# Value means from GpSimd's sums, two casts moved to VectorE, one block of the first x on ScalarE, and one hash a slot earlier, in a fused hash attention and SwiGLU kernel

## The chip, the cores and the metric

The kernel runs on one core of a Trainium2 chip. Such a core has five engines that work side by side, each with an instruction stream of its own in program order: TensorE (PE in the profile; its weight loads are listed as PEld), VectorE (DVE), ScalarE (ACT), GpSimd (POOL) and SyncE (SP), which here only issues DMAs. The engines wait for each other by semaphores. The metric is the device time of one execution, in microseconds. "The median" is that of three runs; the profile is one more execution.

## The reference

```
q, k, v: (4, 8, 768, 64)     batch, heads, sequence, head size; fp32
proj: (64, 6)                w_gate, w_val: (512, 1536)   w_out: (1536, 512)   rms_g: (512,)

bits(t)  = (t @ proj > 0)                        # six bits of each query and key
bucket   = sum(bits * 2**arange(6))
mask     = q_bucket[:, None] == k_bucket[None, :]
scores   = where(mask, q @ k.T / 8, -1e9)
p        = exp(scores - max);   attn = p / (sum(p) + 1e-9)
x        = (attn @ v), the 8 heads side by side          # (3072, 512)
xn       = x / sqrt(mean(x*x) + 1e-6) * rms_g
out      = (silu(xn @ w_gate) * (xn @ w_val)) @ w_out    # (3072, 512)
```

## The kernel before

**Mask.** Nothing is masked by comparison. Each query and key of a head gets six (or twelve) more rows beside its 64 numbers, plus or minus a constant for each hash bit. The product of these rows is largest where all bits agree, so one matmul gives scores in which every other bucket lies far down and vanishes in the exponential. A tile `QK` holds a pair of heads: rows 0 to 63 are the numbers in fp16 (written by casts), the rows from 64 on the hash rows; columns 0 to 767 are queries, the rest keys.

**Means.** A query whose bucket is empty must get the mean of the values, which the small constant `C0` brings in: `v_mean` multiplies the values by a matrix of ones, which sums over the 128 partitions and (with six matmuls into one PSUM bank) over the six blocks of keys, and DVE writes the result, scaled, into `cvb`. Where GpSimd has already added up the six blocks (`v_sum`, into `vsum`), one matmul does. `attn_out` adds `cvb` to the weighted sums before it divides. Before the change batches 0 and 1 use six matmuls for each pair of heads, and batches 2 and 3 use one on GpSimd's sums.

**Units and slots.** A unit `u` is half the queries (384) of a batch; there are eight. A slot is a third of a head: two scores matmuls (L321), one exponential on ACT (`probs`, L333). A unit has 24 slots. The whole program is one list of slots, written out by hand: `at(w, s, f, ...)` appends a step to slot 24*w + s. In slot t the loop emits `scores` of slot t+1, `probs` of slot t, and then the steps of the list in the order in which they were appended. A scores tile has two buffers. The weighted sums (`av`, L346, 18 matmuls a head in two parts) come some slots after their head, into the only bank of their kind; `attn_out` (DVE, then GpSimd) takes them out.

**Filling.** While unit u's attention runs, PE also does unit u-1's gate and value products (`gate`, `value`, L425) and unit u-2's output product (`project`, L454). `spread` lays these pieces over the slots by rough costs (SCORES, AV, PROJ and so on), and puts in the hash of a pair (`hash_one`) at its slot, at the next start of a whole piece. All these matmuls, the hashes (`d_ps`), the transposes of x (`x_ps`) and the means (`m_ps`) share three PSUM banks (`gps`), in rotation. A gate's bank comes free when DVE's first product has read it (L442, `a`), a value's when the second has (L443, `ht`).

**Heads.** Up to pair (1, 1) (batch 1, heads 2 and 3) queries and keys are loaded in rows, turned on PE (`turn_pe`), copied out by DVE or ACT (L152), cast to `QK` on GpSimd (L166), hashed by `hash_direct`, and their hash rows are moved into place by DVE (L251) or sent by DMAs on SP (`send_pair`: L258, then L261). The later pairs are loaded in blocks (`load_blocks`, eight DMAs, and `load_v`, one; all on SP), turned on DVE (`turn_dve`, L176 and L183), cast on GpSimd (L196) and hashed by `hash_one`: eight matmuls (L204), the signs (L212), two selects (L219) and four DMAs on SP (L280). The table `spots` gives for each of these pairs the slot of its load, of its key turns, its query turns and its hash. The casts follow one slot after the turns, and the values' cast and sums (`v_prep`, L289; `v_sum`, L295 to L297) two slots after the last turn; steps that would fall into slots 2 to 6 of a unit move to slot 7. Loaded tiles share eight buffers in rotation, so a load waits until the tile eight before it has been read for the last time. SP works through its DMAs in program order.

**The start.** Pair 0 of batch 0 is set up ahead of the slots: its first head is hashed, and `second_head` (slot 0) does the signs and moves of the second. In slot 1 follow the cast of its values and that of the second half of its queries, both on GpSimd. Units 0 and 1 take turns here: heads 0 and 1 of both come first (`order`).

**The first x.** After the last head of unit 0 a chain runs with nothing beside it that PE could do: the sums are taken out on DVE, squared and reduced (L360 to L388), GpSimd takes the power (L392), DVE scales x (`norm`, L401), PE turns its three blocks (`turn_x`, L408) in slot TX = 37, DVE multiplies them by the weights of the norm (L414), and only then does the first gate matmul start. `turn_x` can also do the multiplication as four on ACT (L412), as it does for one block of the last unit.

Of the kernel before, what the change touches and what calls it, by code (L numbers as in the profile page):

```python
# [31 lines left out]
def kernel(  # L32
# [12 lines left out]
    nc = tc.nc  # L45
# [31 lines left out]
    vls = [const.tile([128, H, 6, 66], FP16, name=f"vl{i}") for i in range(2)]  # L77
# [82 lines left out]
    def turned(b, hp, which):  # L160
        return (qT if which == "q" else kT)[b, hp].rearrange("p (h c) -> p h c", h=2)

    def cast_part(b, hp, which, e, h0=0, n=2):

        o = (0 if which == "q" else S) + e * HALF
        nc.gpsimd.tensor_copy(  # L166
            QK[b, hp][0:64, h0 : h0 + n, o : o + HALF],
            turned(b, hp, which)[64 * e : 64 * e + 64, h0 : h0 + n, :],
        )
# [113 lines left out]
            )  # L283


    def v_prep(b, hp):
        vn = raw[b, hp][2]
        hs = slice(2 * hp, 2 * hp + 2)
        nc.gpsimd.tensor_copy(vls[b % 2][:, hs, :, 0:64], vn)  # L289

    def v_sum(b, hp):
        vn = raw[b, hp][2]
# [244 lines left out]
    NS = 24  # L537
# [5 lines left out]
    def at(w, s, f, *a):  # L543
        plan[NS * w + s].append(lambda: f(*a))
# [7 lines left out]
    sign, move, _ = hash_direct(0, 0, (0,))  # L552
# [9 lines left out]
    sign1, move1, _ = hash_direct(0, 0, (1,))  # L562
# [29 lines left out]
        moves[b, hp][1]()  # L592

    at(0, 0, second_head)
    at(0, 1, v_prep, 0, 0)
    at(0, 1, cast_part, 0, 0, "q", 1)
    for hp, s0 in ((1, 2), (2, 7), (3, 13)):
        at(0, s0, new_pair, 0, hp)
        at(0, s0, turn_pe, 0, hp, 0, "k")
        at(0, s0 + 1, turn_pe, 0, hp, 1, "k")  # L600
        at(0, s0 + 1, cast_pool, 0, hp, "k")
        at(0, s0 + 2, turn_pe, 0, hp, 0, "q", nc.scalar.copy)
        at(0, s0 + 3, turn_pe, 0, hp, 1, "q", nc.scalar.copy)
        at(0, s0 + 3, cast_pool, 0, hp, "q")
        at(0, s0 + 4, hash_pair, 0, hp)
        at(0, s0 + 6, move_pair, 0, hp, 0)
        at(0, s0 + 8, move_pair, 0, hp, 1)
    at(0, 1, load_natural, nc.sync, 0, 3, "k")
    at(0, 1, load_natural, nc.sync, 0, 3, "q")
    at(0, 2, load_v, nc.sync, 0, 2)  # L610
# [12 lines left out]
    for hp, ts in ((0, (8, 22, 23, 24, 25, 24, 26, 26, 28, 42)), (1, (12, 27, 28, 29, 30, 29, 41, 32, 33, 43))):  # L623
        tl, ts = ts[0], ts[1:]
        for w in "kq":
            at(0, tl, load_natural, nc.sync, 1, hp, w)
        at(0, tl, load_v, nc.sync, 1, hp)
        at(0, ts[0], new_pair, 1, hp)
        for t, hh, w in zip(ts[0:4], (0, 1, 0, 1), "kkqq"):
            at(0, t, turn_pe, 1, hp, hh, w)  # L630
        at(0, ts[4], cast_pool, 1, hp, "k")
        at(0, ts[5], cast_pool, 1, hp, "q")
        if hp == 0:
            at(0, ts[6], hash_pair, 1, hp)
            at(0, ts[7], send_pair, 1, hp)
        at(0, ts[8], v_prep, 1, hp)
        at(2, 3 + 6 * hp, v_mean, 1, hp, 2, range(6))

    spots = {
# [11 lines left out]
    TX = 37  # L651
# [8 lines left out]
    at(0, 24, nc.gpsimd.tensor_scalar_mul, gcol, gcol, float(DMODEL) ** 0.5)  # L660
    for n, (u, h) in enumerate(order):
        for part in range(2):
            at(0, 3 * n + 4 + part, av, u, h, part)
        if h % 2:
            if (u, h) == (0, H - 1):

                at(0, 3 * n + 5, o_step, u, h // 2, nc.vector)
                at(0, 3 * n + 5, s_step, u, h // 2)
                at(0, 3 * n + 5, norm_scale, u)
                at(0, 3 * n + 6, hash_only, 1, 1)  # L670
                at(0, 3 * n + 6, hash_signs, 1, 1)
                at(0, 3 * n + 6, norm, u)
                at(0, 3 * n + 7, send_pair, 1, 1)
                at(0, TX - 1, idle, 2, bank)
                at(0, TX, idle, 1, bank)
                for c in range(3):
                    at(0, TX, turn_x, u, c)
                continue
            at(0, 3 * n + 5, o_step, u, h // 2)
            at(0, 3 * n + (10 if h < 7 else 7), s_step, u, h // 2)  # L680
# [1 line left out]

    SCORES, AV, PROJ, FEED, TURN, HASH = 330, 290, 216, 324, 220, 1000
    hashes = {spot[3]: (HASH, hash_one, *pair) for pair, spot in spots.items()}

    def spread(t0, n, pieces):
        fixed = [SCORES + (AV if (t - 1) % 3 < 2 else 0) for t in range(t0, t0 + n)]
        extra = [(t, *hashes.pop(t)) for t in range(t0, t0 + n) if t in hashes]  # L690
        total = sum(fixed) + sum(p[0] for p in pieces) + sum(e[1] for e in extra)
        i, done = 0, 0
        for s in range(n):
            done += fixed[s]
            while i < len(pieces):
                weight, whole, steps = pieces[i]
                if extra and whole and t0 + s >= extra[0][0]:
                    _, weight, *step = extra.pop(0)
                    at(0, t0 + s, *step)
                    done += weight  # L700
                    continue
                if done + weight // 2 > total * (s + 1) // n:
                    break
                done += weight
                for delay, *step in steps:
                    at(0, t0 + s + delay, *step)
                i += 1
        for _, _, *step in extra:
            at(0, t0 + n - 1, *step)
        assert i == len(pieces)  # L710

    for u in range(7):
# [4 lines left out]
        if u == 0:  # L717
            t0 = TX + 1
            spread(t0, 2 * NS - t0, gates)
            continue  # L720
        t0 = NS * (u + 1)
        at(0, t0 + 4, norm, u)
        pieces = []
        for i in range(9):
            c, n = divmod(i, 3)
# [6 lines left out]
                    (TURN, False, [(0, turn_x, u, c)]) for c in ((0,), (1, 2))[i - 6]  # L732
                ]
        spread(t0, NS, pieces + gates)
    for t, (_, *step) in hashes.items():
        at(0, t, *step)

    def behind_norm(t):
# [3 lines left out]
    for (b, hp), (load, kturns, qturns, _) in spots.items():  # L742
        at(0, load, load_blocks, nc.sync, b, hp)
        at(0, load, load_v, nc.sync, b, hp)
        at(0, kturns[0], new_pair, b, hp)
        for w, turns in (("k", kturns), ("q", qturns)):
            for i, t in enumerate(turns):
                at(0, t, turn_dve, b, hp, w, i, len(turns))
            at(0, behind_norm(turns[-1] + 1), cast_pool, b, hp, w)
        t = behind_norm(qturns[-1] + 2)  # L750
        at(0, t, v_prep, b, hp)
        if b > 1:
            at(0, t, v_sum, b, hp)
            at(2 * b, 3 + 6 * hp, v_mean, b, hp, 2)
        else:
            at(2 * b, 3 + 6 * hp, v_mean, b, hp, 2, range(6))


    def head_of(t):
# [61 lines left out]
```

## Time and profile before

| | us |
|---|---|
| median of three runs | 343.63 (342.87 to 345.09) |
| profiled execution | 344.45 |
| its span in the trace | 342.6 |
| PE busy | 329.6 |
| DVE busy | 249.2 |
| ACT busy | 225.6 |
| GpSimd busy | 146.3 |

| group | count | mean ns of one |
|---|---|---|
| scores matmul, 384 columns (L321) | 384 | 326 |
| mean matmul, 130 columns, from the values (L305) | 48 | 220 |
| mean matmul, 130 columns, from GpSimd's sums (L305) | 8 | 225 |
| cast of values on GpSimd (L289) | 16 | 846 |
| the three additions of GpSimd's sums (L295, L296, L297) | 8 each | 1002, 458, 457 |
| multiplication of a turned block of x on DVE (L414) | 23 | 686 |
| the same on ACT, a quarter of a block (L412) | 4 | 369 |

The span is the time from the first to the last instruction of the trace; the execution's own time also holds what lies around it. A matmul's listed time is its way through the pipe. Matmuls overlap, so what one costs PE is the distance from its start to that of the next one: four of 384 columns take 0.65 us, though each is listed with some 0.33. A line of the timeline gives the start, the time that a run of equal instructions takes, the engine, the line of the code and the shapes, how many they are, and in brackets how long the engine sat idle before and what ended that.

### The profile page before, as it was taken

What the parts mean: (1) busy time and instruction counts of PE and PEld (TensorE: products, weight loads), DVE (VectorE), ACT (ScalarE), POOL (GpSimd) and SP (SyncE); (2) the same over time, 40 slices, a digit from 0 to 9 for tenths busy, and PEclk for the clock granted to TensorE, in tenths of its full rate; (3) what the DMA queues carried; (4) which work ended last, traced back from release to release, by engine and by line L of the source; (5) the groups of instructions that cost most, each with busy time, mean ns of one, the idle gap of its engine ahead of it and who ended that gap; (6) DMA issues with size and microseconds to landing.
All of it is one profiled execution on the core that took longest, in us unless ns stands there. A gap on an engine that the chain in (4) does not pass through costs nothing.

```text
span 342.6 us, 7811 instructions
## 1 busy us (share of the span) xinstructions
PE 329.6 (96%) x3030; PEld 197.7 (58%) x3030; DVE 249.2 (73%) x523; ACT 225.6 (66%) x327; POOL 146.3 (43%) x208
## 2 busy tenths in 40 slices
PE   7798989999989999999999999999999999999996
PEld 3465746656656556654656556565556656664554
DVE  3689996778878758976799757986696546674870
ACT  3789866666747667767676667776667867753322
POOL 4589927125343532737362623637281121112000
PEclk9999999999999999999999999999999999999999
DMA  7999947912957017161727027100200010001002
GB/s 228 331 199 287 208 96 118 201 39 45 198 115 140 4 68 151 45 125 50 122 77 140 5 70 129 50 5 26 76 4 6 3 61 33 0 2 61 33 0 94
DMA packets 79029, 31.21 MB, mean 91 GB/s; under 512 B 64928, under 2 KB 75024, under 8 KB 78992
## 3 DMA queue, kind: packets, MB, share of 16 engines
q1 hardware_dynamic: 75888, 25.73, 31.3%
q0 software_dynamic: 2656, 4.72, 7.8%
q8 instruction: 24, 0.39, 0.5%
q10 hardware_dynamic: 448, 0.27, 0.3%
q14 instruction: 13, 0.11, 0.1%
HBM read 28.32 MB, written 6.29 MB: 101 GB/s over the span
## 4 chain that ended last, share of the span: by engine, by line
PE 84%; DVE 10%; ACT 2%; issue 2%; POOL 1%; DMA 1%; DVEq 0%; SPq 0%; POOLq 0%
PE v_ps L425 17%; PE g_ps L425 17%; PE s_ps L321 16%; PE y_ps L454 16%; PE o_ps L346 9%; PE d_ps L204 2%; PE t_ps L150 2%; PE d_ps L229 2%; PE x_ps L408 1%; ACT psb L333 1%; DVE xnT L414 1%; PE m_ps L305 1%; DVE a L442 1%; PE z_ps L525 1%; DVE QK L251 1%
## 5 line engine op out<-in xcount | busy, mean ns | idle before, releaser
L333 ACT ACTIVATE psb<-s_ps,ebias 128x768 f16<-128x768 f32 x192 | 168.1, 901 | 24.3 <-PE s_ps L321 23.5
L321 PE MATMUL s_ps<-QK 76*128 76x384 f16 (+1 forms) x384 | 93.8, 326 | 4.4 <-DVE QK L251 1.9
L433 ACT ACTIVATE t<-g_ps 128x384 f32<-128x384 f32 x96 | 47.2, 491 | 61.7 <-PE g_ps L425 60.9
L425 PE MATMUL g_ps<-xnT,wg 128*128 128x384 f16 x384 | 82.5, 325 | 1.0 <-DVE xnT L414 0.8
L425 PE MATMUL v_ps<-xnT,wv 128*128 128x384 f16 x384 | 81.6, 325 | 0.9 <-DVE a L442 0.8
L442 DVE SCALAR_TENSOR_TENSOR a<-t,g_ps 128x384 f32<-128x384 f32 x96 | 52.7, 548 | 26.9 <-ACT t L433 25.1
L454 PE MATMUL y_ps<-wo,ht 128*128 128x512 f16 x276 | 68.0, 378 | 0.0
L367 POOL TENSOR_TENSOR x<-otmp,rcp 128x384 f32<-128x384 f32 x31 | 25.7, 830 | 98.8 <-DVE rcp L365 98.3
L346 PEld LDWEIGHTS <-psb 128*128 128x128 f16 x1152 | 51.9, 97 | 18.3 <-issue 2.3
L443 DVE SCALAR_TENSOR_TENSOR ht<-a,v_ps 128x384 f16<-128x384 f32 x96 | 53.2, 554 | 11.5 <-PE v_ps L425 2.5
L346 PE MATMUL o_ps<-vl,psb 128*128 128x65 f16 x1152 | 56.3, 193 | 1.0 <-DVE otmp L360 0.9
L321 PEld LDWEIGHTS <-QK 76*128 76x128 f16 (+1 forms) x384 | 34.4, 98 | 37.2 <-issue 11.3
L425 PEld LDWEIGHTS <-wv 128*128 128x128 f16 x384 | 35.2, 97 | 23.3 <-issue 2.5
L425 PEld LDWEIGHTS <-wg 128*128 128x128 f16 x384 | 34.7, 97 | 21.9 <-issue 0.9
L454 PEld LDWEIGHTS <-ht 128*128 128x128 f16 x276 | 24.7, 97 | 22.5
L196 POOL CAST QK<-kT 64x768 f16<-64x768 f32 x20 | 16.4, 822 | 24.9 <-DVE kT L176 11.5
L372 POOL TENSOR_TENSOR sq<-x 128x384 f32<-128x384 f32 x31 | 25.7, 828 | 2.4
L466 ACT COPY ysb<-y_ps 128x512 f32<-128x512 f32 x23 | 13.5, 586 | 18.5 <-PE y_ps L454 18.4
L196 POOL CAST QK<-qT 64x768 f16<-64x768 f32 x20 | 16.6, 831 | 19.3 <-DVE qT L183 18.0
L376 DVE TENSOR_REDUCE ssp<-sq 128x3 f32<-128x384 f32 x32 | 16.9, 529 | 9.7 <-POOL sq L372 9.6
L360 DVE TENSOR_TENSOR otmp<-o_ps,cvb 128x390 f32<-128x390 f32 x32 | 17.9, 558 | 5.9 <-PE o_ps L346 5.6
L414 DVE TENSOR_TENSOR xnT<-x_ps,gcol 128x512 f16<-128x512 f16 x23 | 15.1, 686 | 5.9 <-PE x_ps L408 5.9
(76 smaller groups left out, 275.2 us busy)
## 6 DMA issues: line engine op xcount, KB each, us to landing
vn<-in_v_dram SPq DMA_DIRECT2D x16, 384.0 KB
out_dram<-ysb SPq DMA_DIRECT2D x23, 256.0 KB
qL<-in_q_dram SPq DMA_DIRECT2D x40, 96.0 KB
kL<-in_k_dram SPq DMA_DIRECT2D x40, 96.0 KB
kn<-in_k_dram SPq DMA_DIRECT2D x5, 384.0 KB
qn<-in_q_dram SPq DMA_DIRECT2D x5, 384.0 KB
wg<-in_moe_w_gate_dram POOLq DMA_DIRECT2D x2, 768.0 KB, 10.2
wv<-in_moe_w_val_dram POOLq DMA_DIRECT2D x2, 768.0 KB, 9.7
```

What stands on the lines that cost most here:

```text
L196: nc.gpsimd.tensor_copy(QK[b, 2 * hp + hh, "h"][0:64, o : o + S], src[64 * hh : 64 * hh + 64, :])
L321: nc.tensor.matmul(ps[:, j, 0:HALF], QK[b, h, "h"][0:rows, S + jt * 128 : S + (jt + 1) * 128], QK[b, h, "h"][0:rows, half * HALF : (half + ...
L333: nc.scalar.activation(psb[u, h][:, 2 * ch : 2 * ch + 2, :], sps.pop((u, i))[:, :, 0:HALF], AF.Exp, bias=ebias, scale=ESCALE,)
L346: nc.tensor.matmul(o[:, c, hh, 0:65], psb[u, h][:, jt, c * 128 : (c + 1) * 128], vls[b % 2][:, h, 2 * (jt % 3) + jt // 3 if b in PARITY el ...
L367: eng.tensor_mul(xd.rearrange("p c (h d) -> p c h d", h=2), tmp[:, :, :, 0:64], r.to_broadcast([128, 3, 2, 64]),)
L372: eng.tensor_mul(sq, xd, xd)
L414: nc.vector.tensor_mul(dst, ps, gcol.unsqueeze(2).to_broadcast([128, 4, 128]))
L425: nc.tensor.matmul(ps, w[:, kt, fs], xnT[u][:, kt, :], start=(kt == 0), stop=(kt == 3))
L433: nc.scalar.activation(t, fbank[u, ft, "g_ps"], AF.Tanh, scale=0.5)
L442: nc.vector.scalar_tensor_tensor(out=a, in0=t, scalar=1.0, in1=g, op0=ALU.add, op1=ALU.mult)
L443: nc.vector.scalar_tensor_tensor(out=ht[u][:, ft, :], in0=a, scalar=0.5, in1=vv, op0=ALU.mult, op1=ALU.mult)
L454: nc.tensor.matmul(y, ht[u][:, ft, c * 128 : (c + 1) * 128], wo[:, ft, :], start=(ft == 0), stop=(ft == NF - 1),)
```

## The change

- **Value means.** For batches 1 to 3 GpSimd adds up the six blocks of each pair (batch 1 did not have that before), and two means for four heads each, one matmul of 260 columns, take the place of four means for two heads each. They stand at slots 3 and 18 of the batch's first unit, placed by `spread` like the hashes, with a cost of 120. Batch 0 stays as it was.
- **Pair 0.** The cast of the second half of its queries (slot 1) and the cast of its values (slot 1 before, slot 3 now) are done by DVE instead of GpSimd. The weighted sums of the first head come one slot later, at slots 5 and 6.
- **The first x.** The middle one of unit 0's three blocks is multiplied on ACT. The sending of pair (1, 1)'s hash rows (one DVE instruction, four DMAs) moves from slot 34 to slot 38, behind the x.
- **Hash (1, 3).** Its turns move from slots 57, 58, 59, 60 to 57, 57, 58, 59, and its hash from slot 61 to 60; casts, values' cast and sums follow a slot sooner. Load (2, 1) moves from slot 59 to 62. With the costs in `spread` the hash comes between the two value pieces of slot 60 and gates 3, where it came behind them.

```diff
-    def cast_part(b, hp, which, e, h0=0, n=2):
+    def cast_part(b, hp, which, e, h0=0, n=2, eng=nc.gpsimd):
         o = (0 if which == "q" else S) + e * HALF
-        nc.gpsimd.tensor_copy(
+        eng.tensor_copy(
...
-    def v_prep(b, hp):
+    def v_prep(b, hp, eng=nc.gpsimd):
...
-        nc.gpsimd.tensor_copy(vls[b % 2][:, hs, :, 0:64], vn)
+        eng.tensor_copy(vls[b % 2][:, hs, :, 0:64], vn)
...
-    at(0, 1, v_prep, 0, 0)
-    at(0, 1, cast_part, 0, 0, "q", 1)
+    at(0, 1, cast_part, 0, 0, "q", 1, 0, 2, nc.vector)
...
+    at(0, 3, v_prep, 0, 0, nc.vector)
...
         at(0, ts[8], v_prep, 1, hp)
-        at(2, 3 + 6 * hp, v_mean, 1, hp, 2, range(6))
+        at(0, ts[8], v_sum, 1, hp)
...
-        (1, 3): (45, (57, 58), (59, 60), 61),
+        (1, 3): (45, (57, 57), (58, 59), 60),
...
-        (2, 1): (59, (72, 73, 75, 81), (82, 83, 84, 85), 86),
+        (2, 1): (62, (72, 73, 75, 81), (82, 83, 84, 85), 86),
...
-            at(0, 3 * n + 4 + part, av, u, h, part)
+            at(0, 3 * n + 4 + part + (n == 0), av, u, h, part)
...
-                at(0, 3 * n + 7, send_pair, 1, 1)
+                at(0, TX + 1, send_pair, 1, 1)
...
-                    at(0, TX, turn_x, u, c)
+                    at(0, TX, turn_x, u, c, c == 1)
...
-    SCORES, AV, PROJ, FEED, TURN, HASH = 330, 290, 216, 324, 220, 1000
-    hashes = {spot[3]: (HASH, hash_one, *pair) for pair, spot in spots.items()}
+    SCORES, AV, PROJ, FEED, TURN, HASH, MEAN = 330, 290, 216, 324, 220, 1000, 120
+    inserts = {spot[3]: (HASH, hash_one, *pair) for pair, spot in spots.items()}
+    for b in (1, 2, 3):
+        inserts[2 * b * NS + 3] = (MEAN, v_mean, b, 0, 4)
+        inserts[2 * b * NS + 18] = (MEAN, v_mean, b, 2, 4)
...
         at(0, t, v_prep, b, hp)
-        if b > 1:
-            at(0, t, v_sum, b, hp)
-            at(2 * b, 3 + 6 * hp, v_mean, b, hp, 2)
-        else:
-            at(2 * b, 3 + 6 * hp, v_mean, b, hp, 2, range(6))
+        at(0, t, v_sum, b, hp)
```

More of the change, by code (lines that the diff above doesn't have):

```diff
@@ L680 @@
             at(0, 3 * n + (10 if h < 7 else 7), s_step, u, h // 2)
-    SCORES, AV, PROJ, FEED, TURN, HASH = 330, 290, 216, 324, 220, 1000
-    hashes = {spot[3]: (HASH, hash_one, *pair) for pair, spot in spots.items()}
+    SCORES, AV, PROJ, FEED, TURN, HASH, MEAN = 330, 290, 216, 324, 220, 1000, 120
[3 more added lines that the diff above has]
+        inserts[2 * b * NS + 18] = (MEAN, v_mean, b, 2, 4)
     def spread(t0, n, pieces):
         fixed = [SCORES + (AV if (t - 1) % 3 < 2 else 0) for t in range(t0, t0 + n)]
-        extra = [(t, *hashes.pop(t)) for t in range(t0, t0 + n) if t in hashes]
+        extra = [(t, *inserts.pop(t)) for t in range(t0, t0 + n) if t in inserts]
         total = sum(fixed) + sum(p[0] for p in pieces) + sum(e[1] for e in extra)
@@ L734 @@
         spread(t0, NS, pieces + gates)
-    for t, (_, *step) in hashes.items():
+    for t, (_, *step) in inserts.items():
         at(0, t, *step)
```

## The prediction

> **What bounds the kernel now.** I read the page's busy shares and its chain first, then the waits of PE, then the stretches.
>
> ```profile
> PE 329.6 (96%) x3030; PEld 197.7 (58%) x3030; DVE 249.2 (73%) x523; ACT 225.6 (66%) x327; POOL 146.3 (43%) x208
> ...
> PE 84%; DVE 10%; ACT 2%; issue 2%; POOL 1%; DMA 1%; DVEq 0%; SPq 0%; POOLq 0%
> ```
>
> PE is busy for 96% of the span, and 84% of the chain is PE. So a matmul taken away is time won, and so is a gap of PE that closes; work on another engine costs only where PE waits for it. Where PE waits:
>
> ```profile
> PE s_ps L321 <- DVE QK L251: 1.9, 2, 1.7
> PE s_ps L321 <- DMA QK<-bits: 1.2, 1, 1.2
> ...
> PE g_ps L425 <- DVE xnT L414: 0.8, 1, 0.8
> ```
>
> (us in total, times, longest.) Each has its place: 12.34, 101.37 and 50.87 us. The stretches tell how firmly an early gain holds:
>
> ```profile
> 10.00:50.00 40.00, 36.18 (x473) 24.28 (x472) 34.55 (x72) 34.39 (x45) 29.90 (x37) 1.00 0.94 227
> 50.00:310.00 260.00, 256.29 (x2328) 153.25 (x2327) 193.68 (x406) 177.41 (x256) 110.45 (x140) 1.00 0.33 69
> ```
>
> (Columns: PE, PEld, DVE, ACT, POOL busy, clock, DMA share.) From 50 to 310 us PE has 3.7 us idle and GpSimd 150. From 10 to 50 PE, DVE and ACT are all 86 to 90% busy: there a gain of one engine may stop at the next.
>
> **The change, part by part.**
>
> *Value means.* A mean of six matmuls of 130 columns pushes back what follows by 0.35:
>
> ```profile
> 30.32 0.51 PE L305 MATMUL m_ps<-vl,ones 128*128 128x130 f16 x6
> 30.67 0.49 PE L321 MATMUL s_ps<-QK 70*128 70x384 f16 x2
> ```
>
> That is 58 ns each. Batch 1 loses 24 of them, batches 2 and 3 four each: 32 x 58 = 1.86 us. In come six of 260 columns, a width the trace has not. The bounds are 58 (130 columns) and 163 ns (384 columns, four in 0.65); on the line between, 111, since the neighbouring widths grow evenly: 0.67. Gain **1.2** (0.9 to 1.5). Six bank uses of three rotating banks go as well; at 188.9 and 246.2 the starts of PE's matmuls show gaps of 0.36 ahead of a mean, and one of these places loses its mean: I take **0.1** (0 to 0.4). DVE writes six means of 260 columns for twelve of 130 (0.29 each; 0.55 would be 384 columns): no more than before, not counted. GpSimd gets three additions for each of four pairs, 1.00 + 0.46 + 0.46, 7.7 us in all; its 150 us of idle hide them. Without that cover the mean would wait: the last sums of batch 2 end at 178.2 today, and their mean, now at slot 114, is due near 184 (those of slots 111 and 117 run at 179.4 and 189.6 today). The value tile of pair (1,0) comes free 1.9 us later, and a load behind it on SP waits for that tile already (4.5 us); that load is transposed at 88.9 and was all issued at 66.5.
>
> *Two casts on DVE.* The tiny moves of hash rows show what GpSimd does to them:
>
> ```profile
> 8.08 0.53 DVE L251 TENSOR_SCALAR QK<-bits 6x384 f16<-6x384 f16 x2
> 10.41 0.82 POOL L289 CAST vl<-vn 128x768 f16<-128x768 f32 x1 [1.39 <-DMA vn<-in_v_dram]
> 10.57 1.67 DVE L251 TENSOR_SCALAR QK<-bits 6x384 f16<-6x384 f16 x2
> 11.30 0.83 POOL L166 CAST QK<-qT 64x768 f16<-64x768 f32 x1
> 12.34 0.48 PE L321 MATMUL s_ps<-QK 70*128 70x384 f16 x2 [1.65 <-DVE QK L251]
> 12.86 1.69 ACT L333 ACTIVATE psb<-s_ps,ebias 128x768 f16<-128x768 f32 x2 [0.77 <-PE s_ps L321]
> ```
>
> Two moves take 0.53 at 8.08 and 1.67 at 10.57, and each slow one ends 0.12 after a GpSimd cast does. These two casts are the ones that leave GpSimd. The moves then end 1.1 sooner, at 11.1; next comes ACT, whose second exponential ends at 12.09: scores at 11.35, the third exponential at 12.09 for 12.86, 0.77 won. The Trainium skill says of this (SBUF — State Buffer, "Who interferes with whom") that DVE's two-port operations and GpSimd share a port pair under an exclusive lock, and that whichever starts first makes the other wait; by that rule, the trace agrees with the loss of 1.1, and the same lock can hold DVE's new casts: the second would end at 15.0.
>
> The casts on DVE: 768 elements; by the row of xn (512 elements, 0.48, a new one each 0.37) 0.5 to 0.7, by GpSimd's cast 0.83. I take 0.6. The first follows second_head, which ends 1.1 sooner, and so costs the key copies nothing. The second, at slot 3, starts at 14.0 as GpSimd begins a key cast: it ends at 14.6, or behind that cast at 15.0. The first weighted sums, now at slots 5 and 6 (18 matmuls, the same count), are due at 14.5; scores that came at 16.00 then come at 15.1 to 15.5. I take **0.6** of the 0.77. Bounds: 1.1 if the moves' gain passes whole, and 0.6 lost if the moves are slow for another reason and DVE merely gets a cast more ahead of its key copies.
>
> *First turned x.* Today PE stands still for 0.85 before the first gate:
>
> ```profile
> 48.60 0.42 DVE L258 TENSOR_SCALAR bits<-bits,own 128x768 f16<-128x768 f16 x1
> 48.93 1.88 DVE L414 TENSOR_TENSOR xnT<-x_ps,gcol 128x512 f16<-128x512 f16 x3
> 50.87 0.81 PE L425 MATMUL g_ps<-xnT,wg 128*128 128x384 f16 x4 [0.85 <-DVE xnT L414]
> ```
>
> The hash send (L258) moves behind the x; 0.33 goes. One of three multiplications (0.6 apart) goes to ACT as four, which at the tail take 1.14. DVE then ends at 48.7 + 1.25 = 49.95; ACT, free from 47.95, starts when the middle block is turned (48.75) and ends at 49.9. PE's other work ends at 49.85. Gain **0.85** (0.6 to 1.0). The four stand before probs 38, which moves from 48.0 to 49.9; its scores buffer is next wanted at 52.5, and ACT had 2.84 idle there. The send's four DMAs go out on SP at 50.5 instead of 49, so load (1,3) behind them starts 1.9 later (cover as above); its own reader comes at slot 53, near 80 us.
>
> *Hash (1,3) a slot sooner.*
>
> ```profile
> 93.39 0.87 DVE L176 STREAM_TRANSPOSE qT<-qL 128x384 f32<-128x384 f32 x1
> 94.20 0.51 PE L204 MATMUL d_ps<-kT,pj 128*32 128x384 f32 x1
> 97.20 0.58 SPq L103 DMA_DIRECT2D vn<-in_v_dram  x1
> 97.89 3.40 SPq L280 DMA_DIRECT2D QK<-bits  x4
> 101.37 0.48 PE L321 MATMUL s_ps<-QK 76*128 76x384 f16 x2 [1.19 <-DMA QK<-bits]
> ```
>
> The eight hash matmuls, sign, two selects and four DMAs come one slot (1.9 us) sooner, and the nine DMAs of load (2,1), which SP works off ahead of them today, come behind them. From issue to scores it takes 3.48. Gaps today: 1.35 here and 0.35 before 92.86, together 1.70. But the hash now meets its transposes. With the mean out of slot 57 the first key transpose starts at 88.57, the second 0.71 on; then the rows' spacings give a at 90.06, ht 90.71, qT 91.18 and 91.89, done at 92.76. PE, whose v_ps of slot 59 waits for that a until 90.65, does two scores and two value matmuls and is at the hash at 91.64: **PE waits 1.15 for the transposes**. 1.70 - 1.15 = **0.55** won. The bits are selected by 95.1, or, held by GpSimd's value cast and first sum, which also come a slot sooner, by 96.4; scores can follow at 98.7 to 100.0, and PE is there at 100.0. Bounds: 1.7 if nothing waits; 0.3 lost if the selects are held (two took 1.55 at 155.8 for 0.68 at 96.2) and PE's banks wait with them.
>
> Sum: 1.2 + 0.1 + 0.6 + 0.85 + 0.55 = 3.3. The profiled execution took 344.45 (span 342.6 and 1.85 around it), so 341.15; it lies 0.8 over the median of 343.63. The median less 3.3 is **340.4**.
>
> **The rivals.**
> - *Better*: the hash waits little, because DVE is further ahead once the mean and its 0.29 are out, and the start keeps 1.0: 1.3 + 1.0 + 0.85 + 1.5 = 4.65, 339.0. For it: DVE idles 0.56 before the a of slot 57. Against: today's transposes end only as the hash begins. 0.24.
> - *The start gives nothing*: the change doesn't free the moves, or the second cast meets GpSimd's key cast and the weighted sums wait. 0.6 falls away and up to 0.6 is lost: 341.3 to 341.9, say 341.6. For it: four busy engines from 10 to 50. 0.20.
> - *The hash turns into a wait* of its full price, and the selects are held: 0.85 less, 341.3; with half the start gone 341.9. 0.08.
> - *Slower: load (2,1) comes late.* It starts behind the bits at 98.6 to 99.9. Load (2,2) today starts at 101.34 and its DMA is quiet by 110.5: 9 us. By that (2,1) lands by 109, and its first transpose, today 114.61, comes near 111.5. From a landing after 111.5 on, DVE stands, and PE with its three banks behind it. Load (1,3) took from 51.93 to 66.5 to issue; at that pace (2,1) lands near 115.5 and 4.0 us are lost: 344.4. Against: that load waited 4.5 for a value tile and shared the DMA with weights. 0.06.
>
> **How the numbers follow.** Forecast 0.42, the rivals 0.24, 0.20, 0.08 and 0.06. One per cent, 3.4 us (about what a measurement of this kernel can tell from no change), puts the border at 340.2, just under the forecast. Of its own spread (339.6 to 341.2) some 0.4 lies below: 0.17, with the better case 0.41 faster. Slower than 347 needs the last rival and more: 0.03. The rest, 0.56, is within 1%. The range takes in the better case and the two middle ones: 338.7 to 342.8.
>
> **What would show it.** L305 with 24 matmuls of the first kind and six of 260 columns near 111 ns; the moves at 10.6 at 0.27 each and s_ps at 11.4; the first gate near 49.4 with no wait for xnT; at the hash of (1,3) a wait for DVE qT of about 1, and none for QK<-bits. The prediction is wrong if the gain is gone by 47 us, if PE waits at (2,1)'s transposes, or if gaps open elsewhere as DVE's selects meet the new sums.

## The result, and the profile after

The changed kernel took 341.9 us in the median (341.06 to 342.13, 10 runs) and the kernel before, on the same chip, 345.08 (342.87 to 348.05, 10 runs): a ratio of 0.9912, interval 0.9883 to 0.9941. That is 3.2 us less, where 3.3 less was forecast. Over the 90 runs of the kernel before that were taken beside the experiments below, its median is 344.53; against that the change is worth 2.6 us. The total came near the forecast; its terms did not, as the experiments show.

The profiled execution took 342.05 (span 340.3). From its page, busy shares and the chain:

```profile
PE 331.1 (97%) x3004; PEld 198.0 (58%) x3004; DVE 249.0 (73%) x518; ACT 226.7 (67%) x331; POOL 152.9 (45%) x218
...
PE 88%; DVE 7%; ACT 3%; issue 1%; DVEq 0%
```

The DMA has left the chain, and PE's share of it has grown from 84 to 88%. The waits of PE (us in total, times, longest):

```profile
PE o_ps L346 <- DVE otmp L360: 1.4, 3, 0.6
PE z_ps L525 <- DVE pj L483: 1.2, 1, 1.2
PE s_ps L321 <- ACT psb L333: 1.1, 2, 0.8
PE v_ps L425 <- DVE a L442: 0.6, 1, 0.6
PE s_ps L321 <- DVE QK L251: 0.3, 1, 0.3
```

The waits for the hash rows (QK<-bits) and for the first x (xnT) are gone. The wait for the moves has shrunk from 1.9 to 0.3; in its place PE waits for an exponential (psb, 0.8 at most), as the prediction worked out. The stretches, columns as before:

```profile
10.00:50.00 40.00, 37.06 (x475) 24.28 (x476) 35.42 (x75) 35.20 (x48) 28.69 (x35) 1.00 0.94 219
50.00:310.00 260.00, 258.76 (x2322) 153.84 (x2321) 193.38 (x402) 178.84 (x260) 119.62 (x153) 1.00 0.34 72
```

From 50 to 310 PE now has 1.2 us idle (3.7 before). GpSimd carries the new sums within its idle time.

**Where the time went.** I number the pairs of scores matmuls from 0 and take their starts from the timeline; pair n is emitted in slot n-1. (A pair with one number, such as pair 66, is one of these from here on, and a pair with two, such as (1,3), is one of heads; "pair 0" in the expectations of e2 and e5 is the first pair of heads.) The first column is when pair 0 starts, the others are distances. The later rows are the experiments.

| profiled kernel | pair 0 | 0 to 36 | 36 to 40 | 40 to 60 | 60 to 72 | 72 to last matmul |
|---|---|---|---|---|---|---|
| before | 8.67 | 36.81 | 7.01 | 37.14 | 21.83 | 227.77 |
| changed | 9.49 | 36.34 | 6.18 | 36.61 | 21.03 | 227.30 |
| means alone (e1) | 9.49 | 36.01 | 7.01 | 36.67 | 24.29 | 227.22 |
| casts alone (e2) | 9.50 | 36.28 | 7.01 | 37.14 | 21.63 | 227.82 |
| first x alone (e3) | 9.09 | 38.92 | 6.17 | 37.14 | 22.07 | 227.60 |
| hash and load (e4) | 9.50 | 36.10 | 7.01 | 37.14 | 21.27 | 227.46 |
| spare casts on GpSimd (e5) | 9.14 | 38.93 | 6.18 | 36.63 | 21.05 | 227.25 |
| second mean tripled (e6) | 9.04 | 36.28 | 6.18 | 36.66 | 21.06 | 227.27 |
| hash back at 61 (e7) | 9.01 | 36.29 | 6.18 | 36.62 | 21.02 | 227.23 |
| load back at 59 (e8) | 9.46 | 36.29 | 6.17 | 36.62 | 25.30 | 227.16 |
| load alone (e9) | 8.54 | 36.34 | 7.00 | 37.15 | 20.50 | 227.45 |
| means and load (e10) | 9.39 | 36.02 | 7.01 | 36.62 | 20.63 | 227.52 |
| old turns (e11) | 8.70 | 36.34 | 6.17 | 36.61 | 20.62 | 227.27 |
| old turns, old casts (e12) | 9.23 | 36.00 | 6.18 | 36.62 | 20.61 | 227.27 |

The program is the same in all of them up to pair 0, and yet pair 0 starts anywhere from 8.54 to 9.50. So the 2.28 us between the last matmuls of the two profiles (339.23 and 336.95) hold +0.82 that lies ahead of any edit (the last section says what it goes with), and then -0.47, -0.83, -0.53, -0.80 and -0.47. The distances repeat far better: 36.61 to 36.67 wherever the means are in, 6.17 or 6.18 wherever the x is.

### The profile page after: what moved, and what is told of

It is laid out like the page before. It is cut to its first block, busy times and chain, and to the rows that moved or that the text cites. A ratio compares the mean times of both kernels' runs of the same rounds, so it can differ in the third digit from the quotient of the medians.

```text
span 340.3 us, 7757 instructions
## 1 busy us (share of the span) xinstructions
PE 331.1 (97%) x3004; PEld 198.0 (58%) x3004; DVE 249.0 (73%) x518; ACT 226.7 (67%) x331; POOL 152.9 (45%) x218
## 4 chain that ended last, share of the span: by engine, by line
PE 88%; DVE 7%; ACT 3%; issue 1%; DVEq 0%
PE g_ps L425 18%; PE v_ps L425 17%; PE y_ps L454 17%; PE s_ps L321 17%; PE o_ps L346 9%; PE d_ps L204 3%; PE x_ps L408 2%; DVE QK L251 2%; PE t_ps L150 2%; ACT psb L333 2%; PE d_ps L229 2%; DVE bits L212 1%; PE z_ps L525 1%; DVE a L442 1%; DVE kT L152 1%
```

## The experiments

### Each part alone: e1 to e4

e1 has the new means alone:

```diff
-        at(2, 3 + 6 * hp, v_mean, 1, hp, 2, range(6))
+        at(0, ts[8], v_sum, 1, hp)
...
+    for b in (1, 2, 3):
+        hashes[2 * b * NS + 3] = (MEAN, v_mean, b, 0, 4)
+        hashes[2 * b * NS + 18] = (MEAN, v_mean, b, 2, 4)
...
-        if b > 1:
-            at(0, t, v_sum, b, hp)
-            at(2 * b, 3 + 6 * hp, v_mean, b, hp, 2)
-        else:
-            at(2 * b, 3 + 6 * hp, v_mean, b, hp, 2, range(6))
+        at(0, t, v_sum, b, hp)
```

> The kernel before with the value means of the change alone (GpSimd sums for batch 1, two means for four heads a batch). My theory: PE gets back matmul time, 1.3 us in all, of which 0.9 in batch 1. In the slot-by-slot comparison of the scores' starts with the kernel before, a mean that goes gives back 0.35 and one that comes costs 0.11 in a slot without gates; where it stands among gates (slot 18 of a unit) it costs the 0.35 that the changed kernel shows, because the next gate waits for its bank anyway. Rival: the means were hidden behind DVE and the three banks, so taking them out gives less than 0.5. The wait of 1.2 at pair (1,3)'s hash rows stays, or grows by what PE gains ahead of it (0.6 in slots 51 and 57).

e2 has the two casts on DVE, with the first weighted sums a slot later:

```diff
-    at(0, 1, v_prep, 0, 0)
-    at(0, 1, cast_part, 0, 0, "q", 1)
+    at(0, 1, cast_part, 0, 0, "q", 1, 0, 2, nc.vector)
+    at(0, 3, v_prep, 0, 0, nc.vector)
-            at(0, 3 * n + 4 + part, av, u, h, part)
+            at(0, 3 * n + 4 + part + (n == 0), av, u, h, part)
```

> The kernel before with the two casts of pair 0 on DVE and the first weighted sums a slot later, nothing else. My theory: the two moves of hash rows after the first sign take 0.53 together instead of 1.67, the scores of slot 2 come 0.9 sooner against the start of the scores of slot -1, and of this 0.5 is left at the first gate matmul (0.47 in the changed kernel, once the different start of its matmul clock is taken out). Rival: the busy engines from 10 to 50 us eat all of it, and the first gate comes at the same distance from the first scores as in the kernel before.

e3 has the first x:

```diff
-                at(0, 3 * n + 7, send_pair, 1, 1)
+                at(0, TX + 1, send_pair, 1, 1)
-                    at(0, TX, turn_x, u, c)
+                    at(0, TX, turn_x, u, c, c == 1)
```

> The kernel before with one block of the first x on ACT and the sending of pair (1,1) behind it, nothing else. My theory: the gap of 0.85 before the first gate closes, the scores after it come 0.83 sooner, and the gain stays until the end of the program but for what the hash rows of pair (1,3) take back: their DMAs hang on DVE and SP, which gain as well, so at least 0.6 of 0.83 is left at the end. Rival: the whole gain is lost again at that wait, since PE reaches it sooner and the rows come no sooner.

e4 has the line of spots, hash and load together:

```diff
-        (1, 3): (45, (57, 58), (59, 60), 61),
+        (1, 3): (45, (57, 57), (58, 59), 60),
-        (2, 1): (59,
+        (2, 1): (62,
```

> The kernel before with the turns and the hash of pair (1,3) a slot sooner and load (2,1) three slots later, nothing else. My theory: the wait of 1.2 for the hash rows goes, and the hash itself is stretched by 1.0, since its query products wait for the transposes; net gain 0.4 at the scores of slot 65. Rival A: without the removed mean in slot 57 DVE is later and the hash waits longer, net 0 or a loss. Rival B: the hash waits little and the gain is over 1.

| kernel | median (range) us | ratio to before, interval |
|---|---|---|
| e1 means | 345.24 (343.42 to 347.32) | 1.0028 (0.9997 to 1.0058) |
| e2 casts | 344.62 (343.95 to 345.23) | 1.0009 (0.9987 to 1.0031) |
| e3 first x | 343.64 (343.29 to 346.21) | 0.9993 (0.9966 to 1.0021) |
| e4 hash and load | 343.27 (342.97 to 344.92) | 0.9974 (0.9954 to 0.9993) |

Added up, the four parts give +0.04%; together they give -0.88%. Much of that gap is the granted clock: seven of e1's ten runs, three of e3's and one of e4's have a mean clock of 0.995 or less, and none of e2's or of the changed kernel's. The runs at full clock (0.998 or more) have medians of 343.42 (e1, three runs only), 344.62, 343.43 and 343.20, where those of before on this chip have 344.39. These differences add up to -2.9 us, about what the four edits give together. So what the parts lack when they stand alone is above all runs without a drop of the clock.

e2 and e4 went as expected in their profiles. In e2 pairs 0 to 3 take 2.78 for 3.67, and 0.53 of that is left at pair 36; the time gained nothing even so, and e12 tells why. In e4 the hash is stretched to 1.87, the rows go out 0.07 after the selects, and pair 66 comes 0.56 sooner, counted from pair 40 (0.4 was expected).

The trace of e1 shows a gain that is lost. Its means win what they should until pair 60 (36.67 for 37.14) and another 0.48 at slot 64. Then, in the timeline of e1, SP and PE:

```profile
89.43 5.05 SPq L117 DMA_DIRECT2D qL<-in_q_dram  x4
94.58 2.94 SPq L117 DMA_DIRECT2D kL<-in_k_dram  x4
97.62 0.58 SPq L103 DMA_DIRECT2D vn<-in_v_dram  x1
98.31 3.40 SPq L280 DMA_DIRECT2D QK<-bits  x4
...
101.96 0.49 PE L321 MATMUL s_ps<-QK 76*128 76x384 f16 x2 [2.74 <-DMA QK<-bits]
```

The hash rows of (1,3) are ready when their second select ends, at 96.40 (two selects: 0.67 from 95.73). SP sends them at 98.31, for it issues load (2,1) first, whose four qL alone take 5.05. The load starts 36.9 after pair 40, as in the profile of before, though PE is half a microsecond ahead by then. So what PE has gained since pair 40 only makes its wait longer: 2.74 for 1.19 before. And the wait costs more than itself. The stretches of e1:

```profile
98.00:102.00 4.00, 1.26 (x16) 0.64 (x12) 2.02 (x5) 1.76 (x3) 3.53 (x6) 1.00 0.61 146
102.00:106.00 4.00, 4.00 (x23) 2.25 (x24) 1.67 (x4) 1.28 (x2) 0.00 (x0) 0.57 0.65 103
```

After it the granted clock is 0.57 for four microseconds, and PE runs 23 matmuls there where before ran 38. The seven runs with the lower mean clock took 345.15 to 347.32, the three at full clock 343.42 to 343.61; how long PE waited in those three, no trace shows. The profile of e3, its slowest run (346.21), shows a drop at the start:

```profile
12.00:16.00 4.00, 3.81 (x16) 2.85 (x17) 2.42 (x7) 2.33 (x3) 0.43 (x1) 0.50 0.74 260
16.00:20.00 4.00, 4.00 (x44) 2.43 (x43) 0.04 (x1) 3.28 (x5) 3.48 (x5) 0.64 0.57 129
```

That is its 38.92; it has nothing to do with the x, whose own step (7.01 to 6.17) is as forecast. Of the 0.84 of this step e3 loses 0.24 at the hash rows, where PE waits 1.46: the load starts 36.9 after pair 40 here too, so a gain ahead of that pair brings it forward, and most of the gain passes.

### The load back at 59, and the hash back at 61: e8 and e7

Both start from the changed kernel. e8:

```diff
-        (2, 1): (62,
+        (2, 1): (59,
```

> The changed kernel with load (2,1) back at slot 59, ahead of the hash rows of pair (1,3) on SP. If the order on SP is needed for the gain: the hash rows go out after the load's last DMA, 1 us or more later than in the changed kernel (97 instead of 94.9), and PE waits up to 0.9 at the scores of slot 65. If the hash's own slot is enough: the load is through by then, the rows go out within 0.3 of the selects and nothing is lost.

e7:

```diff
-        (1, 3): (45, (57, 57), (58, 59), 60),
+        (1, 3): (45, (57, 57), (58, 59), 61),
```

> The changed kernel with the hash of pair (1,3) back at slot 61, but its turns still a slot sooner and load (2,1) still behind it. My theory: the hash no longer meets its transposes (0.87 us instead of 1.85, 1.0 won), and the hash rows, which go out at once since no load is ahead of them, come at 98.8 to 99.7 by the changed kernel's clock; PE reaches the scores of slot 65 at 98.6, so it waits 0.2 to 1.1 there: between 0.8 faster and no difference. Rival (the slot is what counts): the full wait of 1.2 for the rows is back, the kernel is slower than the changed one.

e8 took 343.28 (342.95 to 346.12), ratio 0.9974 (0.9955 to 0.9994): of the change's 0.88% only 0.26% is left, though the means, the x and the sooner hash are all in. e7 took 341.81 (341.24 to 342.16), ratio 0.9924 (0.9899 to 0.9949), the same as the changed kernel. The timeline of e8, SP and PE (this profile is the slowest of its nine runs and the only one with a lower mean clock; the other eight took 342.95 to 343.78):

```profile
88.89 6.40 SPq L117 DMA_DIRECT2D qL<-in_q_dram  x4
...
98.83 3.39 SPq L280 DMA_DIRECT2D QK<-bits  x4
...
102.62 0.80 PE L321 MATMUL s_ps<-QK 76*128 76x384 f16 x2 [3.06 <-DMA QK<-bits]
```

Its selects end at 94.80, and the rows wait four microseconds for their turn on SP, longer than was expected. The load's place is worth 1.4 us in the medians, 2.1 by the ratios. The hash's slot by itself is worth nothing: in e7, as in the changed kernel, 60 to 72 takes 21.02. In e7 the hash isn't stretched (0.79 from its first matmul to the next scores), but the 1.0 that was to be won so is lost elsewhere. Its two query transposes stand together from 90.01 to 91.57, ahead of the first product `a`, and PE waits for that:

```profile
92.01 0.48 PE L425 MATMUL v_ps<-xnT,wv 128*128 128x384 f16 x2 [0.73 <-DVE a L442]
```

In e11 below, with the old turns, this wait is 0.18.

### The load alone, with the means, and the old turns: e9, e10, e11

e9 is the kernel before with the load's slot as its only edit; e10 has the means as well; e11 is the changed kernel with the old spots of pair (1,3).

```diff
-        (2, 1): (59,
+        (2, 1): (62,
```

> The kernel before with load (2,1) at slot 62 in place of 59 and nothing else; turns and hash of (1,3) stay where they were. Theory (what holds back a lead of PE at slot 65 is the order of SP's DMAs: load (2,1) stands ahead of the four DMAs of the hash rows): these go out within 1 us of the second select, near 96.5 to 97 instead of 97.9, s_ps(66) waits at most 0.5 for QK<-bits instead of 1.2, the hash is not stretched, and the time is 0.5 to 1.3 under the kernel before. Rival (the slot of the hash is what counts, the load is a side matter): the rows still go out after 97.5, the wait stays near 1.2, and the time is within 0.4 of the kernel before.

> The kernel before with the new means and load (2,1) at slot 62, turns and hash of (1,3) as before. The means alone gave nothing in the time, since their lead of about 1 us at slot 65 met a wait of 2.7 us for the hash rows. Theory (order on SP): with the load behind the rows this wait is under 1 us, and the means' 1.2 to 1.4 pass to the end beside what the load gives alone: 1.7 to 2.7 under the kernel before, and more than 1 under the load alone. Rival (the lead is lost for another reason, for instance at the banks or at DVE): within 0.6 of the load alone.

```diff
-        (1, 3): (45, (57, 57), (58, 59), 60),
+        (1, 3): (45, (57, 58), (59, 60), 61),
```

> The changed kernel with turns and hash of (1,3) back at slots 57, 58, 59, 60 and 61; load (2,1) stays at slot 62. Theory (order on SP; the hash's own slot is worth what it wins less what its transposes cost, about 0.4): within 0.6 of the changed kernel on either side, the hash no longer stretched by 1, a wait for QK<-bits of 0.3 to 1.3 in its place. Rival (the prediction's account, the slot of the hash wins 1.7 and loses 1.15): 0.5 to 0.8 over the changed kernel; if the whole price comes back, 1.5 or more over it.

| kernel | median (range) us | ratio to before, interval |
|---|---|---|
| e9 load | 342.73 (342.04 to 345.2) | 0.994 (0.9906 to 0.9973) |
| e10 means and load | 342.36 (341.82 to 342.63) | 0.9926 (0.99 to 0.9951) |
| e11 old turns | 341.32 (340.75 to 341.66) | 0.9888 (0.9847 to 0.9929) |

One number in the code, 59 to 62, gives 2.0 us (before: 344.72 on this chip). The timeline of e9, DVE, SP and PE:

```profile
95.59 0.68 DVE L219 TENSOR_SCALAR bits<-bits,sel 128x384 f16<-128x384 f16 x2
...
96.33 3.42 SPq L280 DMA_DIRECT2D QK<-bits  x4
```

The rows go out 0.06 after the second select, PE waits no more for them, and 60 to 72 takes 20.50 for 21.83. This is more than was expected of it, and the hash stands where it stood: the order on SP is what held pair 66 back. With the load behind them the rows also land a little sooner: where PE waits for them, the scores follow the first row's issue by 3.11 to 3.14 with the load at 62 (e7, e10 to e12), and by 3.18 to 3.79 with it at 59 (before, e1 to e3, e8).

e10 was expected to bring 1.7 to 2.7 under before and more than 1 under the load alone. The first holds (2.36), the second doesn't: 0.37, which is what the rival said (within 0.6). The means win 0.53 from pair 40 to 60, but after that hardly anything. At slot 64 PE is 0.48 further ahead, and it then waits 0.38 for the hash rows, whose hash lies before that mean and so was not brought forward by it. From 60 to 72 e10 is 0.13 longer than e9, and from 72 on 0.07.

e11 tells what the sooner turns and hash are worth: 60 to 72 takes 20.62 without them and 21.03 with them (21.02 to 21.06 in e5, e6 and e7, which all have the sooner turns). They cost 0.41, and e7, which differs from e11 only in the turns and the casts behind them, says that it is the turns; without the means they cost more, 0.77 (e4 against e9). The timeline of the changed kernel, DVE, PE with its weight loads, and SP:

```profile
90.49 1.58 DVE L176 STREAM_TRANSPOSE qT<-qL 128x384 f32<-128x384 f32 x2
...
91.04 0.83 PE L204 MATMUL d_ps<-kT,pj 128*32 128x384 f32 x2
...
92.12 0.14 PEld L204 LDWEIGHTS d_ps<-qT,pj 128*32 128x32 f32 x2 [0.57 <-DVE qT L176]
92.12 0.83 PE L204 MATMUL d_ps<-qT,pj 128*32 128x384 f32 x2
92.89 0.50 PE L321 MATMUL s_ps<-QK 76*128 76x384 f16 x2
...
94.91 3.41 SPq L280 DMA_DIRECT2D QK<-bits  x4
```

and of e11, PE alone:

```profile
92.38 0.51 PE L204 MATMUL d_ps<-kT,pj 128*32 128x384 f32 x1
...
93.26 0.50 PE L321 MATMUL s_ps<-QK 76*128 76x384 f16 x2
...
98.25 0.48 PE L321 MATMUL s_ps<-QK 76*128 76x384 f16 x2 [0.37 <-DMA QK<-bits]
```

From the first hash matmul to the next scores it takes 1.85 in the changed kernel and 0.88 in e11. The missing 0.97 is the wait for the query transposes, the last of which ends at 92.07. The rows of PE's matmuls list no wait there, since a query matmul that waits lies between key matmuls that don't; those of its weight loads (PEld) list two, 0.24 at 91.41 and the 0.57 above. In e11 PE waits 0.37 for the rows instead. By the medians e11 is 0.6 better than the changed kernel, by the ratios 0.0024, and the intervals overlap; the distances, which repeat to 0.04 with the sooner turns and to 0.02 without (e10 to e12), settle it.

### What the casts are worth: e5 and e12

e5 adds to the changed kernel two casts on GpSimd of the size of the values' cast, into a tile that nobody reads:

```diff
+    def spare_casts():
+        for _ in range(2):
+            nc.gpsimd.tensor_copy(spare, raw[0, 0][2])
+    at(0, 1, spare_casts)
     at(0, 1, cast_part, 0, 0, "q", 1, 0, 2, nc.vector)
```

> The changed kernel with two more casts on GpSimd in slot 1 (the values of pair 0, 128 x 768, twice, into a tile that nothing reads); they stand where the two casts stood before. They share no output with anything. My theory (GpSimd holds DVE off while it runs): the two moves of hash rows that meet them take about 1.6 us instead of 0.53, each ending about 0.1 after a cast, and the scores of slot 2 come about 0.8 later. Rival (the moves waited for what the casts wrote, or for something else): the moves stay at 0.27 each and the scores come as in the changed kernel.

It took 342.11 (341.56 to 344.31), ratio 0.9925 (0.9902 to 0.9948). The timeline of the changed kernel at the moves:

```profile
11.39 0.53 DVE L251 TENSOR_SCALAR QK<-bits 6x384 f16<-6x384 f16 x2
...
12.27 0.48 PE L321 MATMUL s_ps<-QK 70*128 70x384 f16 x2 [0.76 <-ACT psb L333]
...
14.79 0.56 DVE L289 CAST vl<-vn 128x768 f16<-128x768 f32 x1
14.82 2.10 POOL L166 CAST QK<-kT 64x768 f16<-64x768 f32 x2 [4.97 <-DVE kT L152]
```

and of e5 (its lines are one later, by the new tile):

```profile
10.48 1.71 POOL L599 CAST spare<-vn 128x768 f16<-128x768 f32 x2 [0.99 <-DMA vn<-in_v_dram]
...
11.04 1.26 DVE L252 TENSOR_SCALAR QK<-bits 6x384 f16<-6x384 f16 x2
...
12.40 0.80 PE L322 MATMUL s_ps<-QK 70*128 70x384 f16 x2 [1.25 <-DVE QK L252]
```

With casts on GpSimd beside them the moves take 1.26 (1.6 was expected), without them 0.53. So the casts hold the moves. In the other direction DVE's cast at 14.79 holds GpSimd's at 14.82: the two take 2.10, where they take 1.70 in e12, which has no cast of DVE beside them. This is what the Trainium skill says (SBUF — State Buffer, "Who interferes with whom"): DVE's two-port operations and GpSimd share a port pair under a lock, and whichever starts first blocks the other. The trace agrees in both directions.

But how long the moves are held depends on when the values land, counted from the moves, and the profile of before was an extreme case. All kernels with both casts on GpSimd:

| profile | values' cast starts | moves start | two moves take | pair 0 to 3 |
|---|---|---|---|---|
| before | 10.41 | 10.57 | 1.67 | 3.67 |
| e9 | 9.53 | 10.44 | 1.20 | 3.20 |
| e3 | 9.98 | 10.99 | 1.09 | 3.09 |
| e1 | 10.18 | 11.39 | 0.90 | 2.90 |
| e10 | 10.04 | 11.29 | 0.88 | 2.88 |
| e12 | 9.81 | 11.13 | 0.88 | 2.88 |
| e4 | 9.79 | 11.39 | 0.54 | 2.79 |

In before the moves start 0.16 after the first cast, and each of the two casts holds one of them. In the others they start 0.91 to 1.60 after it, when it is over, and only what is left of the second cast holds them: they end 0.38 to 0.43 after that cast does.

With the casts on DVE pair 0 to 3 is 2.78 in every profile (3.27 in e5). Against that, pairs 3 to 36 take 33.50 to 33.56 with them (without e5) and 33.11 to 33.14 without (33.31 in e4; 35.83 in e3, whose clock fell): some 0.4 more. Between e12 and e11, which differ in the casts alone, 0.43 of it opens at pair 24. There PE's weighted sums wait 0.25 in e11 for DVE's `otmp`. DVE falls behind ahead of that, where two later moves of hash rows take 1.90 in e11 (at 27.38) and 1.28 in e12 (at 28.16); why they are held longer isn't shown. So the casts on DVE win 0.89 and lose 0.4 in a run like the profile of before, and lose up to 0.3 in runs like those of e1, e10 and e12. This was tested last, by e11 without the casts:

```diff
-    at(0, 1, cast_part, 0, 0, "q", 1, 0, 2, nc.vector)
+    at(0, 1, v_prep, 0, 0)
+    at(0, 1, cast_part, 0, 0, "q", 1)
-    at(0, 3, v_prep, 0, 0, nc.vector)
-            at(0, 3 * n + 4 + part + (n == 0), av, u, h, part)
+            at(0, 3 * n + 4 + part, av, u, h, part)
```

> The kernel before with the means, the first x and load (2,1) at slot 62: neither the two casts on DVE (with the weighted sums a slot later) nor the sooner hash. Between the first scores and those of slot 35 the profiled kernels with the two casts on GpSimd took 36.81 (before), 36.01, 36.34, 36.10 and 36.02 us, and with the casts on DVE 36.28 to 36.34. Theory from this (the casts win only where the values land so late that GpSimd's two casts cover the moves, as in the profile of before; elsewhere they cost up to 0.3): 36.0 to 36.8 here, the move of hash rows held for 0.5 to 1.7, and the median within 0.4 of the kernel with the casts and the old turns (ratio .9888). Rival (the prediction: the casts win 0.5 to 0.6 in every run): 0.5 or more over that kernel. With both edits left out the ratio is then .987 to .990 by the theory, above .990 by the rival.

It took 341.23 (340.9 to 343.82), ratio 0.989 (0.9845 to 0.9934), with 36.00 from pair 0 to 36 and the two moves at 0.88. All of this is as expected. The median is that of e11: the casts don't move it. Their use may be another one. Of the 39 runs of e4, e9, e10 and e12, with the casts on GpSimd and no long wait for the hash rows, five have a mean clock of 0.995 or less, and the one of e12 is its 343.82; of the 39 of the changed kernel, e2, e6, e7 and e11 none has. A shorter wait at the moves would explain it, but only e3 and e5 have a profile with that drop at the start, so it stays a guess.

### The second mean tripled: e6

```diff
-            nc.tensor.matmul(
-                ps, ones16, rhs, start=(i == 0), stop=(i == len(parts) - 1)
-            )
+            for _ in range(times):
+                nc.tensor.matmul(
+                    ps, ones16, rhs, start=(i == 0), stop=(i == len(parts) - 1)
+                )
...
-        inserts[2 * b * NS + 18] = (MEAN, v_mean, b, 2, 4)
+        inserts[2 * b * NS + 18] = (MEAN, v_mean, b, 2, 4, (None,), 3)
```

> The changed kernel with the second mean of each of batches 1 to 3 (slot 18 of the unit, among gates) multiplied three times over, each result written over the one before: two more matmuls of 260 columns, 0.22 us of PE time, at three places. My theory: the next gate waits for its bank 0.24 behind the mean, so most of the 0.22 is hidden: under 0.1 lost at each place, under 0.3 in all. Rival (the price of a mean is its matmul time): 0.22 lost at each, 0.67 in all.

It took 341.74 (341.62 to 342.08), ratio 0.9933 (0.9911 to 0.9956), and its distances are those of the changed kernel to 0.06. Six more matmuls of 260 columns cost nothing: in the changed kernel the gate starts 0.35 after such a mean, in e6 0.35 after the first of three, for it waits for its bank, not for PE. In e6 the three stand 0.111 to 0.115 apart, so the prediction's price for this width (111 ns) was right; it is of no weight at these three places.

## Why the prediction was right or wrong

- **What bounds the kernel**: right. Every gain and loss above is a matmul taken out or a gap of PE opened or closed.
- **Value means, 1.2 and 0.1**: too high. The matmuls went as forecast (L305 has 24 of 130 columns and six of 260), each of these six costs the 111 ns of the forecast (e6), and the means of slots 51 and 57 won 0.24 and 0.35. But the sum took 58 ns for each matmul as if PE were the bound at every mean. At slot 64 the lead ran into the hash rows (0.13 lost between 60 and 72), and in batches 2 and 3 a mean displaces a gate by 0.35 to 0.45 that waits for a bank anyway, and gives as much back later. From 72 on the nine kernels with the means take 227.28 on average, the five without 227.62, but the one clean pair (e9, e10) shows none of that 0.34. Together 0.4 to 0.75. The medians leave it as wide: 0.37 between e9 and e10, 0.97 for e1's three runs at full clock.
- **Two casts on DVE, 0.6**: the mechanism is right and the size true of the profile that it was read from (36.81 to 36.34, 0.47; the moves at 0.53; at 14.8 DVE's cast does meet a GpSimd cast, though it is GpSimd's that is held). The step that failed is to take one profile's start for the typical one. Over the profiles with full clock the distance is 36.00 to 36.81 without the casts, 36.21 on average, and 36.28 to 36.34 with them. The rival "the start gives nothing" was the true one, and its 341.6 the nearest to the 341.9 measured, for another reason than it gave first: not that the moves stay slow, but that all six other profiles with the casts on GpSimd hold them less. Its second reason, that the casts meet, did come true; whether the 0.4 lost behind pair 3 comes of it isn't shown.
- **First turned x, 0.85**: right, 0.83. The rows came as worked out; the timeline of the changed kernel has

```profile
48.95 1.28 DVE L414 TENSOR_TENSOR xnT<-x_ps,gcol 128x512 f16<-128x512 f16 x2
49.20 1.15 ACT L412 ACTIVATE xnT<-x_ps,gcol 128x128 f16<-128x128 f16 x4 [0.78 <-PE x_ps L408]
...
50.38 0.81 PE L425 MATMUL g_ps<-xnT,wg 128*128 128x384 f16 x4
```

- **Hash (1,3), 0.55**: the size is right where the edit stands alone (e4, 0.56), the account isn't. The wait for the transposes was worked out at 1.15 and measured 0.97. But the 1.70 of gaps was put to the hash's sooner slot and the load's move together, as if the first were needed. The load's move alone closes 1.33 of it (e9), and the sooner turns and slot take 0.41 back with the means in (e11), 0.77 without them (e4 against e9). In the changed kernel that makes 0.93 between 60 and 72 (the 0.80 measured and the 0.13 that the means lose there).
- **The sum, 3.3**: with the casts at 0, the distances from pair 36 on add up to 0.83 + 0.53 + 0.80 + 0.47 = 2.63, and the medians of all runs give 2.6. Of the 2.63 the x has 0.83, hash and load 0.93 and the means 0.4 to 0.75; the rest, 0.1 to 0.5, all behind pair 72, no run assigns. So the forecast was 0.7 too high, and as near as that only by luck: hash and load brought more than their term while casts and means brought less.
- **The time, 340.4**: 1.5 too low. It was counted from a median of three runs, 343.63; with ten runs on one chip it was 345.08, and with 90 344.53. So 0.9 of the error is the start of the count and 0.7 the sum.
- **The rival "slower: load (2,1) comes late"**: refuted. No wait of PE appears at its transposes in any kernel with the load at 62. That this load stood in the way, the prediction said in half a sentence, and priced only the danger of moving it.
- **That terms of one sum are independent** was never questioned. The row of 97.89 in the profile of before showed a DMA that left 1.0 after its data was ready; it fixes pair 66 against what PE gains shortly before it. The means of slots 51, 57 and 64 lost their lead there in e1's profile, and the clock with it, so in such a run their term hung on the load's edit; what e1's three runs at full clock did there isn't known. The gains ahead of pair 40 hung on it less (e3 lost 0.24 of its 0.84 there, e2 nothing).

## What to carry to other kernels

Before gains are added up along an engine, look for a point on its path that is fixed by something else, here a DMA behind a long load in SP's order: a gain shortly ahead of it turns into a longer wait, a long wait may cost the clock as well, and its removal may be worth more than any other edit (here 2.0 us by the medians). Read a start-up phase from several profiles, since what collides there hangs on when a load happens to land. And try the plain edit by itself: the kernel with the load moved, the means and the x, without the sooner hash (e11, e12), beats the changed kernel by 0.6 in the medians and by 0.41 in the distances.

## What the runs showed of the hardware

- **Both waits of PE near 3 us were followed by a halved clock.** After 2.74 (e1) and 3.06 us (e8) the granted clock was 0.57 on average from 102 to 106, and 0.50 for 3.4 us of that; after 1.19 (before) and 1.5 (e3) it stayed at 1.00 there. At the start, waits of 1.07 (e3) and 1.25 (e5) were followed by 0.50 for 6.8 us from 12 on, one of 1.65 (before) by none. The Trainium skill (TensorE: Matmul & The Clock Gate, "Part 1: The HAM clock gate") puts the drop to half after an idle window of some 3.4 us, and calls the window free-running, so that the same kernel varies from run to run. The length of the drops, one and two such windows, and the variation agree. That the window is idle doesn't: in the 3.41 us ahead of the drop PE was busy for 0.67 (e1), 0.89 (e8), 2.21 (e3) and 2.02 (e5), and e3 had 1.95 from 100.77 to 104.18 without a drop. What decides it, these runs don't show.
- **Four DMAs of a load held SP for 4.94 to 6.40 us** (qL of load (2,1) at 89 to 91 us: before, e1 to e3, e8), where the same four took 2.69 at 99.80 in e9. The DMA engines were busy for 0.99 to 1.03 of the time from 88 to 94 in e1, and for 0.38 from 100 to 102 in e9.
- **PE's first scores vary by 0.96 us** between profiles of the same instructions (8.54 to 9.50), more than the x is worth. In thirteen of the fourteen profiles they come the later, the later the trace's record of the clock shows full speed for the first time: 4.05 us in e9, 4.32 in before, 6.90 in the changed kernel, 7.06 in e4. e2 (4.74 and 9.50) is the exception.
